# FFN first half by seven one-lane products in Strassen's way, with V fetched per step

## The chip, the cores and the metric

The kernel runs on one core of one Trainium2 chip. The time is the device time of one execution in microseconds (us); for the kernel before it is the median of three runs. TensorE (PE) multiplies, VectorE (DVE), ScalarE (ACT) and GpSimd (POOL) work on SBUF and PSUM, and SyncE (SP) issues nearly all DMAs.

## What is computed

```python
x = A_x                                   # 2048 x 512, fp32
g = sigmoid((x * gate_w).sum(-1))
qkv = x @ wqkv                            # 32 heads of 16
p = softmax(q @ k.T / 4); o = p @ v       # per head, no mask
a = o @ wo
h = silu(x @ w1) * (x @ w3)               # 2048 x 1792
b = h @ w2
out = g * a + (1 - g) * b
```

All is fp32. The projections and the FFN split each operand into a rounded part (hi) and the rest (lo), and sum three products: hi x hi, lo x hi and hi x lo.

## The kernel before

A first phase of 85 us loads and transposes x, projects the first q and k and all of V, and computes a bound for the softmax. V stays in SBUF for all heads. Then comes one long loop over 1024 score units. A unit is two heads, 128 keys and 512 queries: two matmuls into PSUM (L719), one exp on ACT (L723), and later four matmuls of P times V into four column groups of one bank (L706). A step is the 32 units of one head pair and one half of the queries; after it `evac` copies the bank (L687) and SP stores eight pieces (L693, L700). There are 64 steps.

The order of PE's work is a string written out by hand. Q is a score; F is a slot for two filler matmuls, one on rows 0 to 63 of the array (the upper lane) and one on rows 64 to 127 (the lower lane); P is one unit's PV part, 4 matmuls of 2 heads each taking the time of some slots. A long period is `"QFFF" * 7 + "QPPPP"` (8 scores, 21 slots), and there are 83 of them; a short one is `"QFFF" * 5 + "QPPQQPP"` (8 scores, 15 slots, PV in two pairs), and there are 44. Positions below are counted in such periods.

The fillers are the rest of the kernel, taken in order from `blocks`: the projections of the other q and k, gate and up of the FFN (`w_product`, L409), the second half of the FFN (`h_product`, L518), and part of the output projection (L597). A block has 12 lane matmuls on each lane for K = 512 (four K tiles, three terms), and both lanes sum into one bank: the upper lane takes the first 64 rows of every K tile, the lower lane the other 64. An FFN chunk is one group of 128 columns f of w1 and of w3; it makes eight blocks (gate and up for four blocks of 512 tokens).

When a gate block is done, DVE copies it (L432), ACT takes exp at the next P (L437), and DVE adds one (L438) and takes eight reciprocals (L440), a few per score. The up block is multiplied by the gate (L454), and by the reciprocals (L458), and SP stores that to `h_d` (L459). Weights are loaded by SP (L314) and split by POOL with a cast (L321) and a subtraction (L322). `load_w2` and `load_piece` bring w2 and h back (L487), and POOL splits these too (L488, L489). SP runs its DMAs in program order, so a store that waits for its data holds up every load behind it.

## Time and profile before

| | |
|---|---|
| median of three runs | 1419.17 us (1418.86 to 1424.47) |
| the profiled execution | 1419.55 us |
| its span | 1417.6 us |
| mean granted clock of PE | 1.0 |
| PE, ACT, DVE, POOL busy | 1408.8, 1033.2, 449.4, 321.1 us |
| bytes moved | 141.42 MB in 112668 packets |

A page of the profile gives the busy time of each engine over the span, the chain of work that ended last, and groups of instructions by line with their mean duration, the idle time before them and what ended it. A timeline row gives start and duration in us, the engine, the line, the operation with its tiles, and in brackets the idle time before it. A row of windows gives the stretch, its length, the busy time of PE, PEld, DVE, ACT and POOL, then the granted clock, the DMA share and GB/s. A row of the chain gives start, length, engine and line. A row of waits gives who waited for whom: the total in us, how often, and the longest.

### The profile page before, as it was taken

The page shows a single profiled execution, that of the slowest core. Times are in us where ns is not written, and L with a number is a line of the kernel's source. Part 1 is how long each engine was busy: PE and PEld are TensorE (multiplying, and loading weights), DVE is VectorE, ACT ScalarE, POOL GpSimd, SP SyncE. Part 2 cuts the span into 40 slices and gives each one's busy share as a digit, 9 for nine tenths or more (in the row PEclk, how much of TensorE's full clock was granted, in tenths as well). Part 3 has the DMA queues.
Part 4 walks back from the last instruction along what each step waited for, and adds up shares of the span by engine and source line. Part 5 has one row for each costly group of instructions (what it writes and reads, how often), then busy time and mean ns, then how long its engine had stood idle before and what let it go on. Part 6 is the DMA issues. An engine that isn't in the chain of part 4 may idle for free.

```text
span 1417.6 us, 28518 instructions
## 1 busy us (share of the span) xinstructions
PE 1408.8 (99%) x11399; PEld 833.7 (59%) x11399; DVE 449.4 (32%) x845; ACT 1033.2 (73%) x1153; POOL 321.1 (23%) x356
## 2 busy tenths in 40 slices
PE   9999999999999999999999999999999999999998
PEld 7865656656556566565565665655555555554556
DVE  4421102464555545455464545400000000000013
ACT  4556767777777777777777777777788778877870
POOL 5014443011011100110110015441332332233230
PEclk9999999999999999999999999999999999999999
DMA  7554455342124432223233234543534443345445
GB/s 197 141 121 114 126 140 128 73 110 69 46 61 85 113 69 61 70 72 87 68 76 79 76 81 122 136 101 74 126 81 102 104 105 70 66 112 106 106 133 182
DMA packets 112668, 141.42 MB, mean 100 GB/s; under 512 B 16400, under 2 KB 70672, under 8 KB 109456
## 3 DMA queue, kind: packets, MB, share of 16 engines
q1 hardware_dynamic: 110384, 135.72, 39.6%
q10 hardware_dynamic: 2144, 3.80, 0.8%
q8 instruction: 92, 1.51, 0.5%
q14 instruction: 48, 0.39, 0.1%
HBM read 90.70 MB, written 48.76 MB: 98 GB/s over the span
## 4 chain that ended last, share of the span: by engine, by line
PE 93%; POOL 0%; DMA 0%; DVE 0%; ACT 0%; issue 0%; SPq 0%; ACTq 0%; POOLq 0%
PE acc L706 32%; PE f L409 27%; PE S L719 19%; PE f L518 11%; PE f L597 1%; PE f L95 0%; PE f L97 0%; PE f L96 0%; DMA fr<-in_B_w_dram 0%; PE S L97 0%; PE S L96 0%; PE S L95 0%; POOL xL L489 0%; POOL fl L489 0%; DVE sg L458 0%; POOL xH L488 0%
## 5 line engine op out<-in xcount | busy, mean ns | idle before, releaser
L723 ACT ACTIVATE p<-S 128x1024 f32<-128x1024 f32 x1024 | 967.5, 1026 | 308.4 <-PE S L719 307.1
L706 PE MATMUL acc<-p,V 128*17 128x512 f32 x4096 | 473.5, 594 | 0.0
L719 PE MATMUL S<-Qt,Kt 50*128 50x512 f32 x2048 | 427.9, 413 | 1.1 <-POOLq L278 0.6
L719 PEld LDWEIGHTS S<-Qt,Kt 50*128 50x128 f32 x2048 | 193.8, 184 | 187.4 <-ACT p L723 80.4
L706 PEld LDWEIGHTS acc<-p,V 128*17 128x17 f32 x4096 | 102.8, 97 | 274.1 <-issue 273.9
L409 PE MATMUL f<-xL,fh 64*128 64x512 f32 x1024 | 205.1, 391 | 0.0
L409 PE MATMUL f<-xH,fl 64*128 64x512 f32 x1024 | 204.9, 390 | 0.0
L409 PE MATMUL f<-xH,fh 64*128 64x512 f32 x1024 | 204.7, 390 | 0.0
L440 DVE RECIPROCAL sg<-sg 128x64 f32<-128x64 f32 x448 | 201.2, 509 | 1.9
L409 PEld LDWEIGHTS f<-xL,fh 64*128 64x128 f32 x1024 | 99.4, 187 | 21.2
L409 PEld LDWEIGHTS f<-xH,fl 64*128 64x128 f32 x1024 | 98.5, 185 | 20.1
L409 PEld LDWEIGHTS f<-xH,fh 64*128 64x128 f32 x1024 | 99.4, 187 | 17.7
L321 POOL CAST fh<-fr 128x512 fp32r<-128x512 f32 x32 | 21.6, 674 | 371.1 <-DMA fr<-in_B_w_dram 246.5
L687 DVE COPY u<-acc 128x512 f32<-128x512 f32 x32 | 22.1, 692 | 257.0 <-PE acc L706 257.0
L518 PE MATMUL f<-xH,fl 64*128 64x512 f32 x224 | 82.2, 391 | 0.5 <-POOL fl L489 0.5
L518 PE MATMUL f<-xL,fh 64*128 64x512 f32 x224 | 82.2, 391 | 0.3 <-POOL xL L489 0.3
L518 PE MATMUL f<-xH,fh 64*128 64x512 f32 x224 | 82.1, 391 | 0.0
L518 PE MATMUL f<-xH,raw 64*128 64x512 f32 x192 | 74.9, 390 | 0.0
L532 DVE TENSOR_SCALAR gs<-f,omg 128x512 f32<-128x512 f32 x16 | 12.0, 751 | 176.4 <-PE f L518 176.4
L432 DVE COPY gs<-f 128x512 f32<-128x512 f32 x56 | 38.7, 691 | 78.1 <-PE f L409 78.1
L518 PE MATMUL f<-xH,fr 64*128 64x512 f32 x160 | 62.4, 390 | 0.0
L454 DVE TENSOR_TENSOR raw<-f,gs 128x512 f32<-128x512 f32 x50 | 34.1, 682 | 82.7 <-PE f L409 82.7
(216 smaller groups left out, 1309.6 us busy)
## 6 DMA issues: line engine op xcount, KB each, us to landing
Kt<-kH_d SPq DMA_DIRECT2D x128, 128.0 KB
h_d<-sg SPq DMA_DIRECT2D x56, 256.0 KB
sg<-h_d SPq DMA_DIRECT2D x43, 256.0 KB
fr<-in_B_w_dram SPq DMA_DIRECT2D x42, 256.0 KB
Qt<-qH_d SPq DMA_DIRECT2D x128, 64.0 KB
Kt<-kL_d SPq DMA_DIRECT2D x64, 128.0 KB
fr<-in_A_wqkv_dram SPq DMA_DIRECT2D x18, 256.0 KB
Qt<-qL_d SPq DMA_DIRECT2D x64, 64.0 KB
```

The source lines that it names most:

```text
L321: nc.gpsimd.tensor_copy(wh, r)
L409: nc.tensor.matmul(ps, w[i == 2][r, k, :], (xL if i == 1 else xH)[b][r, k, :], start=n == 0 and r.start == 0, stop=n == 3 * ND - 1 and r.s ...
L432: nc.vector.tensor_copy(gs, ps)
L440: small.append(lambda q=q: nc.vector.reciprocal(sg[:, q:q + 64], sg[:, q:q + 64]))
L454: nc.vector.tensor_mul(gu, ps, st["gs"])
L518: nc.tensor.matmul(ps, hs[t][q][i == 2][r, P * o:P * o + P], (w2L if i == 1 else w2H)[q][r, o, :], start=n == 0 and r.start == 0, stop=n = ...
L532: nc.vector.tensor_scalar(y, ps, omg[:, t:t + 1], None, op0=OP.mult)
L597: nc.tensor.matmul(ps, ot[t][i == 2][r, P * k:P * k + P], wo_[k][i == 1][r, :], start=n == 0 and r.start == 0, stop=n == 3 * ND - 1 and r. ...
L687: nc.vector.tensor_copy(u, acc)
L706: nc.tensor.matmul(acc[r:r + DH + 1, :], V[:, k, 2 * j + h, :], p[:, h, :], start=k == 0, stop=k == NT - 1)
L719: nc.tensor.matmul(ps[:, h, :], Kt[i][r:r + 50, P * k:P * k + P], Qt[i][r:r + 50, t:t + 512], start=True, stop=True)
L723: nc.scalar.activation(p, ps, AF.Exp, scale=SCALE)
```

## The change

The eight one-lane products of a chunk and a pair of token blocks (two token blocks, gate and up, two halves of each K tile) become seven products of sums, 12 lane matmuls each. Every product stands on one lane alone: `f_job` (L631 in the changed kernel) gives four products of a chunk to one lane and three to the other, in turn. There are 28 chunks now: 14 groups of columns for tokens 0 to 1023, then the same for tokens 1024 to 2047. Lane matmuls of the first half go from 2688 to 2352. `chunk_load` issues six loads for a chunk (L593 to L595), a half of them into the other partitions; `chunk_sums` makes four sums on POOL (L602) and `chunk_split` four casts (L617) and four subtractions (L619). Sums of x are made once per half by `x_sums` on DVE and split on POOL (L497, L498); those of the later half wait in DRAM (`X_d`). The outputs are put together on DVE from PSUM (`p1_done` to `p4_done`); the two products of the activation (L673, L687) are on POOL, and the store of h (L688) is on SP.

V goes to DRAM in the first phase (`keep_v`); `load_v_step` (L246) fetches a head pair for each step, 14 scores ahead of it. Pools of tiles are laid out anew. The projections come in another order, w2 is loaded when the last chunk's products end (`f_job`), into the tiles that x leaves, and `h_product` (L765) is emitted when the load of its row of w2 has been emitted. The first half's divisions come later. Of the 127 periods 71 are long; the other 56 have 13 or 14 slots.

```diff
-    V = vp.tile([P, NT, H, DH + 1], F32, name="V")
+    Vt = [vp.tile([P, NT, 2, DH + 1], F32, name=f"Vt{i}") for i in range(2)]
+    ones = const.tile([P, H], F32, name="ones")
     Qt = [qkp.tile([P, S // 2], F32R, name=f"Qt{i}") for i in range(2)]
...
+    def keep_v(t, e):
+        nc.gpsimd.tensor_copy(Vt[0][:, t, :, :], Vs[t][:, 0:2, :])
+        e.dma_start(V_d[t], Vs[t])
...
+    def load_v_step(s):
+        j = s % NPAIR
+        nc.sync.dma_start(Vt[s % 2], V_d[:, :, 2 * j:2 * j + 2, :].rearrange("t p h d -> p t (h d)"))
...
+    def x_sums(half, k):
+        b = 2 * half
+        m, ms = raw(), raw()
+        for i in range(2):
+            nc.vector.tensor_add(m[:, i, :], xH[b + i][:, k, :], xL[b + i][:, k, :])
+        yield
+        nc.sync.dma_start(ms[LO], m[UP])
+        nc.sync.dma_start(ms[UP, 1, :], m[LO, 1, :])
+        for _ in range(3):
+            yield
+        s1, s3 = slot("sg"), slot("sg")
+        nc.vector.tensor_add(s1, m[:, 1, :], ms[:, 1, :])
+        nc.vector.tensor_sub(s3[UP], m[UP, 0, :], m[UP, 1, :])
+        yield
+        nc.vector.tensor_sub(s3[LO], ms[LO, 1, :], ms[LO, 0, :])
+        nc.vector.tensor_add(m[LO, 0, :], m[LO, 0, :], ms[LO, 0, :])
+        yield
+        nc.vector.tensor_sub(m[:, 0, :], s1, m[:, 0, :])
+        yield
+        return s1, m[:, 0, :], s3
...
+    def first_half():
+        assert "saved" in free_x
+        for k in range(ND):
+            s1, s2, s3 = yield from x_sums(0, k)
+            if k == ND - 1:
+                prepare(0)
+            x_split(s1[UP], xH[2][UP, k, :], xL[2][UP, k, :])
+            yield
+            x_split(s3, xH[3][:, k, :], xL[3][:, k, :])
+            yield
+            t = slot("AC"[k % 2], F32R), slot("BD"[k % 2], F32R)
+            x_split(s2, *t)
+            yield
+            for i, xs in enumerate((xH, xL)):
+                nc.sync.dma_start(xs[2][LO, k, :].bitcast(F32), t[i][LO].bitcast(F32))
+            upper_s2.append(t)
+            if 1 in free_x:
+                put_s2()
+        x_there.update((1, 3))
+        for n in (0, 1, 3, 2):
+            chunk_split(chunks[0], n)
+        second_chunk()
...
+    def second_chunk():
+        if 0 in free_x and "a" in chunks[0]:
+            prepare(1)
+            for n in (0, 1, 3, 2):
+                chunk_split(chunks[1], n)
...
+    def chunk_load(c):
+        a, b = raw(), raw()
+        c["a"], c["b"] = a, b
+        for i, w in enumerate((w1, w3)):
+            w = w[:, P * c["f"]:P * c["f"] + P].rearrange("(k p) n -> p k n", p=P)
+            to = lambda t: t[:, i, :].rearrange("p (k n) -> p k n", n=P)
+            nc.sync.dma_start(to(a), w)
+            nc.sync.dma_start(to(b)[UP], w[LO] if i else w[UP])
+            nc.sync.dma_start(to(b)[LO], w[UP])
+    def chunk_sums(c):
+        a, b = c["a"], c["b"]
+        def step(op, to, x, y):
+            def go():
+                op(to, x, y)
+                c["t"] += 1
+            return go
+        sub, add = nc.gpsimd.tensor_sub, nc.gpsimd.tensor_add
+        poolq.extend([step(sub, b[LO, 0, :], a[LO, 0, :], b[LO, 0, :]),
+                      step(sub, b[:, 1, :], b[:, 1, :], a[:, 1, :]),
+                      step(sub, a[UP, 1, :], a[UP, 1, :], a[UP, 0, :]),
+                      step(add, b[:, 0, :], b[:, 1, :], b[:, 0, :])])
+    def chunk_split(c, n):
+        def hi():
+            assert c["t"] == 4
+            c[n] = halves()
+            nc.gpsimd.tensor_copy(c[n][0], src)
+        def lo():
+            nc.gpsimd.tensor_sub(c[n][1], src, c[n][0])
+            c["is", n] = True
+        src = (c["a"], c["a"], c["b"], c["b"])[n][:, (0, 1, 0, 1)[n], :]
+        poolq.extend([hi, lo])
...
+    def f_job(i, n, lane, done, when=None):
+        c = chunks[i]
+        def product(ps, r, m):
+            k, j = divmod(m, 3)
+            nc.tensor.matmul(ps, c[n][j == 2][r, P * k:P * k + P], (xL if j == 1 else xH)[XT[n]][r, k, :],
+                             start=m == 0, stop=m == 3 * ND - 1)
+        def end(ps):
+            done(c, ps)
+            if lane is LO or n == 3:
+                if i + 2 < len(chunks):
+                    chunk_split(chunks[i + 2], n)
+                else:
+                    t = i + 2 - len(chunks)
+                    loads.append(lambda q=len(asked[t]): load_piece(t, q))
+                    asked[t].append(n)
+            if c["half"] == 0 and c["f"] >= NF - (2 if n == 3 else 1):
+                x_from(n, lane)
+            if (c["half"], c["f"], lane) == (1, NF - 1, LO):
+                w = (0, 1, 3, 2)[n]
+                loads.extend([lambda f=f: load_w2(f) for f in range(4 * w, min(4 * w + 4, NF))])
+        def begin():
...
-                nc.vector.tensor_mul(sg, gu, sg)
-                nc.sync.dma_start(h_d[P * f:P * f + P, 512 * b:512 * b + 512], sg)
...
-            if f == NF - 1:
-                loads.extend([lambda c=c: load_w2(c) for c in range(4 * b, min(4 * b + 4, NF))])
-                if b == NB - 1:
-                    loads.extend([lambda q=q: load_piece(1, q) for q in range(2)])
-                    hurry = True
...
+            hurry = hurry or i == len(chunks) - 1
+            if n == 0 and lane is UP and i + 2 < len(chunks):
+                chunk_load(chunks[i + 2])
+            c[n, lane is LO] = True
+            if n == 2 and lane is UP and i + 2 < len(chunks):
+                chunk_sums(chunks[i + 2])
...
+        def silu():
+            nc.gpsimd.tensor_mul(c["sg", b], c["sg", b], gs)
+            ready_h(c, b)
+        soon.append(exp)
+    def ready_h(c, b):
+        c["n", b] = c.get(("n", b), 0) + 1
+        if c["n", b] == 2:
+            poolq.append(lambda: h_out(c, b))
+    def h_out(c, b):
+        sg, f, t = c["sg", b], c["f"], 2 * c["half"] + b
+        h = sg if b else c["up", b]
+        nc.gpsimd.tensor_mul(h, c["up", b], sg)
+        nc.sync.dma_start(h_d[P * f:P * f + P, 512 * t:512 * t + 512], h)
...
+    def p1_done(c, ps):
+        c["A"] = slot("A")
+        nc.vector.tensor_copy(c["A"], ps)
+    def p2_done(c, ps):
+        nc.vector.tensor_add(c["A"], ps, c["A"])
+        assert "B" in c
+        gate(c, 0, c["A"])
+    def p6_done(c, ps):
+        c["B"] = slot("B")
+        nc.vector.tensor_add(c["B"], ps, c["A"])
...
     def load_w2(f):
         if f % 4 == 0:
-            w2H.append(xp.tile([P, 4, 512], F32R, name=f"xH{f // 4}"))
-            w2L.append(xp.tile([P, 4, 512], F32R, name=f"xL{f // 4}"))
-        halves_of(w2[P * f:P * f + P, :], w2H[-1][:, f % 4, :], w2L[-1][:, f % 4, :], "fr")
+            w2H.append(xp.tile([P, 4, 512], F32R, name=f"xH{(0, 2, 3, 1)[f // 4]}"))
+            w2L.append(xp.tile([P, 4, 512], F32R, name=f"xL{(0, 2, 3, 1)[f // 4]}"))
+        halves_of(w2[P * f:P * f + P, :], w2H[-1][:, f % 4, :], w2L[-1][:, f % 4, :], "ww")
+        w2_there.append(f)
...
-    LONG, MID = 83, 0
+    LONG, MID = 71, 28
...
-    two = ["QFFF" * 5 + "QPPQQPP", "QFFF" * 6 + "PPQQPP"]
+    two = ["QQFFFFFQFFFQFFFFFQQPPQQPP", "QFFQFFFFQFFFQFFFFQFQPPQQPP"]
...
+            if issued % 32 == 18 and step < 2 * NPAIR:
+                load_v_step(step)
```

Two places of the new order, the first on SP and POOL. On SP where the FFN begins: `ww` tiles with 64- or 128-row sources from w1 and w3 are the first chunk's operands (`ww_7548`, `ww_7549`), `ww_7531` a block of k, `u` the evacuation of a step.

```order
480 L956 DMA d_d_89<-u_7509 1x512 x4
481 L963 DMA o_d_87<-u_7509 16x512 x4
482 L199 DMA kH_d_83<-ww_7531 128x512
483 L199 DMA kL_d_84<-ww_7531 128x512
484 L565 DMA xH1_236<-A_7076 64x512
...
489 L565 DMA xL1_237<-B_7402 64x512
490 L593 DMA ww_7548<-in_B_w1_dram 128x4x128
491 L594 DMA ww_7549<-in_B_w1_dram 64x4x128
492 L595 DMA ww_7549<-in_B_w1_dram 64x4x128
493 L593 DMA ww_7548<-in_B_w3_dram 128x4x128
494 L594 DMA ww_7549<-in_B_w3_dram 64x4x128
495 L595 DMA ww_7549<-in_B_w3_dram 64x4x128
```

The same weights were two loads per chunk before; here the six loads stand behind two stores of k, eight stores of the evacuation and six moves of sums of x (L565).

On POOL, what stands ahead of the first chunk's first operand, `wt_7637`, of which PE takes the rounded part first (the first product, `f0_7743<-xH0_154,wt_7637`, stands six scores into period 13):

```order
161 L602 TENSOR_TENSOR ww_7549<-ww_7548,ww_7549 64x512
162 L497 CAST xH3_611<-sg_7476 128x512
163 L498 TENSOR_TENSOR xL3_612<-sg_7476,xH3_611 128x512
164 L602 TENSOR_TENSOR ww_7549<-ww_7549,ww_7548 128x512
165 L497 CAST C_7584<-ww_7418 128x512
166 L498 TENSOR_TENSOR D_7585<-ww_7418,C_7584 128x512
167 L602 TENSOR_TENSOR ww_7548<-ww_7548 64x512
168 L461 CAST ww_7625<-ww_7625 128x512
169 L462 TENSOR_TENSOR ww_7625<-ww_7625 128x512
170 L602 TENSOR_TENSOR ww_7549<-ww_7549 128x512
171 L617 CAST wt_7637<-ww_7548 128x512
172 L619 TENSOR_TENSOR wt_7637<-ww_7548,wt_7637 128x512
```

Before, POOL had a cast and a subtraction for each of two tiles at this place (L321, L322); now four sums (L602), the sums of x (L497, L498), a block of k (L461, L462) and the split stand in one row.

On SP where the second half begins, before (`fr` tiles hold rows of w2 or pieces of h):

```order
728 L487 DMA fr_14809<-in_B_w2_dram 128x512
729 L487 DMA fr_14850<-in_B_w2_dram 128x512
730 L487 DMA fr_14884<-in_B_w2_dram 128x512
731 L459 DMA h_d_86<-sg_14729 128x512
732 L487 DMA fr_14913<-in_B_w2_dram 128x512
733 L487 DMA fr_14944<-h_d_86 128x4x128
734 L487 DMA fr_14987<-h_d_86 128x4x128
735 L487 DMA fr_15020<-in_B_w2_dram 128x512
736 L459 DMA h_d_86<-sg_14876 128x512
737 L487 DMA fr_15052<-in_B_w2_dram 128x512
738 L487 DMA fr_15079<-in_B_w2_dram 128x512
739 L487 DMA fr_15122<-in_B_w2_dram 128x512
```

and now, where `ww` tiles hold them and `sg_15491`, `D_15579` and `sg_15789` are products of h of the last two chunks:

```order
936 L688 DMA h_d_86<-sg_15491 128x512
937 L734 DMA ww_15569<-in_B_w2_dram 128x512
938 L734 DMA ww_15588<-in_B_w2_dram 128x512
939 L734 DMA ww_15604<-in_B_w2_dram 128x512
940 L734 DMA ww_15621<-in_B_w2_dram 128x512
...
945 L734 DMA ww_15707<-in_B_w2_dram 128x512
946 L688 DMA h_d_86<-D_15579 128x512
947 L734 DMA ww_15727<-in_B_w2_dram 128x512
...
955 L734 DMA ww_15853<-in_B_w2_dram 128x512
956 L688 DMA h_d_86<-sg_15789 128x512
957 L734 DMA ww_15867<-in_B_w2_dram 128x512
```

The loads of w2 and the stores of h stood mixed over several periods before; now the first load of w2 (row 0) stands behind the store of `sg_15491`, that of row 7 behind the store of `D_15579`, and that of row 13 behind the last store.

On PE the first product that needs row 0 of w2 (`f1_15592<-xH0_15567`, L765) stands one score behind that load in the order of the program; products of the last chunk (L631) run beside it on the other lane, as L409 ran beside L518 before.

More of the change, by code (lines that the diff above doesn't have):

```diff
@@ new lines, in both, with prepare @@
+    def both(*a):
+        upper.append(block(*a))
+        lower.append(upper[-1])
+    def prepare(i):
+        chunk_load(chunks[i])
+        chunk_sums(chunks[i])
+    for c, b in [(c, b) for b in (2, 3) for c in (1, 2, 3)] + [(1, 1), (1, 0), (2, 1), (3, 1), (2, 0), (3, 0)]:
+        for i in range(2):
+            begin = None
+            if (b, i) == (2, 0) and c < ND - 1:
+                begin = lambda c=c: load_weights(c + 1)
+            both(w_product(c, i, b), qk_done(c, i, b), 3 * ND, begin)
@@ L683, in feed @@
+            t["n"] += 1
+            if t["n"] == t["length"]:
+                now[name] = None
+                if t["two"] and name == "upper":
+                    t["up"] = issued
+                else:
+                    t["done"](t["ps"])
+                    ended += 1
+                    left_at[t["bank"]] = clock
         return did
@@ L770, in gated_mix_kernel @@
     assert not pend and issued == 64 * NPAIR
-    assert state_f["upper"] is None and all(b[0] < issued for b in ready)
+    assert not upper and now["upper"] is None and all(t["up"] < issued for t in lower)
     for _ in reciprocals(ND - 1, 1):
```

400 lines of the change are left out of this document (227 added, 173 removed).

## The prediction

> **What bounds the kernel now.** I read the page first, then the chain of waits, then timelines of a long period, a short period and the stretch where the first half of the FFN ends, and last the waits of SP.
>
> ```profile
> span 1417.6 us, 28518 instructions
> PE 1408.8 (99%) x11399; PEld 833.7 (59%) x11399; DVE 449.4 (32%) x845; ACT 1033.2 (73%) x1153; POOL 321.1 (23%) x356
> PE 93%; POOL 0%; DMA 0%; DVE 0%; ACT 0%; issue 0%; SPq 0%; ACTq 0%; POOLq 0%
> L723 ACT ACTIVATE p<-S 128x1024 f32<-128x1024 f32 x1024 | 967.5, 1026 | 308.4 <-PE S L719 307.1
> ```
>
> PE is the bound: busy 99% of the span, 93% of the chain, and ACT idles 308 us waiting for it. So the time is a count of matmul slots times their length, plus whatever makes PE wait. The run that was profiled took 1419.55 us around its span of 1417.6; the median of the three runs is 1419.17, 0.4 below.
>
> A period is 8 scores with the fillers between them. The chain shows the PV blocks, one to a long period:
>
> ```profile
> 104.75 3.56 PE acc L706 x32
> ...
> 241.07 3.56 PE acc L706 x32
> ```
>
> Between them lie 13 periods in 136.32 us: 10.49 each. The slot is read from a timeline of PE:
>
> ```profile
> 602.14 0.40 PE L409 MATMUL f<-xH,fh 64*128 64x512 f32 x2
> 602.38 0.40 PE L409 MATMUL f<-xL,fh 64*128 64x512 f32 x2
> 602.61 0.40 PE L409 MATMUL f<-xH,fl 64*128 64x512 f32 x2
> 602.85 0.40 PE L719 MATMUL S<-Qt,Kt 50*128 50x512 f32 x2
> ...
> 603.78 0.40 PE L719 MATMUL S<-Qt,Kt 50*128 50x512 f32 x2
> ```
>
> Four slots take 0.93 us, so a slot (a pair of fillers, or a score) takes 0.2325. A long period has 8 scores and 21 fillers: 29 x 0.2325 = 6.74, and the rest, 3.75, is the PV block. The exps beside two PV pairs give a short period:
>
> ```profile
> 1099.93 1.94 ACT L723 ACTIVATE p<-S 128x1024 f32<-128x1024 f32 x2 [1.25 <-PE S L719]
> 1109.35 1.94 ACT L723 ACTIVATE p<-S 128x1024 f32<-128x1024 f32 x2 [1.25 <-PE S L719]
> ```
>
> The start of the second row is 9.42 us after the first: 23 slots are 5.35, the PV part 4.08.
>
> **The change part by part.** *PE work.* 83 long and 44 short periods become 71 long, 28 of 21 slots and 28 of 22. Removed: 12 x 10.49 + 44 x 9.43 = 540.8. Added: 28 x (21 x 0.2325 + 4.08) + 28 x (22 x 0.2325 + 4.08) = 28 x 8.96 + 28 x 9.20 = 508.5. The gain is 32.3 us (29 to 34: some of the new periods start with two scores in a row). ACT needs 8 x 1.026 = 8.2 us of 8.96, so it does not become the bound there. Seven products for eight alone would be an eighth of the first half; the fillers that remain set the rest.
>
> The old kernel loses some time itself where the second half starts:
>
> ```profile
> 911.60:934.10 22.50, 21.73 (x160) 12.61 (x161) 1.06 (x2) 15.47 (x18) 10.31 (x12) 1.00 0.31 87
> ```
>
> Two periods and a bit take 1.5 us more than 2 x 10.49. This place is rebuilt, so these 1.5 us go and new waits come.
>
> *Durations off PE.* The new sums, splits and products run on GpSimd (POOL) and stand behind DMAs of SP:
>
> ```profile
> L422 POOL TENSOR_TENSOR gs<-gs,sg 128x512 f32<-128x512 f32 x24 | 30.9, 1289 | 1.9
> L421 POOL CAST sg<-gs 128x512 fp32r<-128x512 f32 x24 | 14.7, 612 | 82.5 <-DVE gs L420 82.5
> L440 DVE RECIPROCAL sg<-sg 128x64 f32<-128x64 f32 x448 | 201.2, 509 | 1.9
> L432 DVE COPY gs<-f 128x512 f32<-128x512 f32 x56 | 38.7, 691 | 78.1 <-PE f L409 78.1
> L438 DVE TENSOR_SCALAR sg<-sg 128x512 f32<-128x512 f32 x56 | 27.1, 484 | 103.0 <-ACT sg L437 103.0
> L437 ACT ACTIVATE sg<-gs 128x512 f32<-128x512 f32 x56 | 35.0, 625 | 0.0
> ```
>
> Between two POOL instructions lie 0.07 us, as the chain shows where two follow each other:
>
> ```profile
> 916.79 0.62 POOL xH L488
> 917.41 0.07 issue
> 917.48 1.28 POOL xL L489
> ```
>
> Two loads show what a load costs from its issue on SP to the cast on POOL:
>
> ```profile
> 198.47 1.03 SPq L314 DMA_DIRECT2D fr<-in_B_w_dram  x2
> ...
> 202.48 0.61 POOL L321 CAST fh<-fr 128x512 fp32r<-128x512 f32 x1 [4.41 <-DMA fr<-in_B_w_dram]
> ```
>
> ```profile
> 889.12 0.37 SPq L487 DMA_DIRECT2D fr<-in_B_w_dram  x1
> 891.79 0.61 POOL L488 CAST xH<-fr 128x512 fp32r<-128x512 f32 x1 [11.98 <-DMA fr<-in_B_w_dram]
> ```
>
> So 4.0 us for the weight columns (x2 issues in 1.03) and 2.7 for a row block of w2; one issue takes about 0.4.
>
> *Start of the FFN.* The six loads of the first chunk (after's L593 to L595) are behind two stores of k, eight evacuations and six moves of x sums. From the first score of that period: 3.75 (PV) + 0.9 + 0.7 (copy) + 16 issues x 0.4 + three of the chunk's own (1.2) + 4.0 = 17 us until the first sum can run; then POOL does eight tensor-tensors and four casts up to the first low part: 8 x 1.29 + 4 x 0.61 + 12 x 0.07 = 13.6. The high part is there after 17 + 12.2 = 29.2. PE meets its first product (L631) one period and 6 scores later: 10.49 + 3.75 + 5 x 0.93 + 2 x 0.23 = 19.4. It waits 29.2 - 19.4, about 9.5 us, and 0.5 at a later operand: 10 (6, if the evacuations are issued while SP would otherwise wait, to 12).
>
> *Second chunk.* Its loads follow the last k store out of the same buffer: copy 0.7, three POOL instructions 3.3, two issues 0.8, the store 2.7 (as the w2 row), six issues 2.4, landing 4.0, three sums 4.1, cast 0.7: 18.7 us after the last projection product. PE wants it 13.5 us after (one period and 13 slots): a wait of 5 (2 to 8).
>
> *End of the FFN's first half.* Before, most loads of w2 are issued periods ahead, and yet one of them already ended in the chain, behind a store of h:
>
> ```profile
> 909.52 0.69 DVE hx L454
> 910.21 0.47 DVE sg L440
> ...
> 910.70 1.28 DVE sg L458
> ...
> 912.00 0.32 SPq L459
> ...
> 912.42 4.25 DMA fr<-in_B_w_dram
> ```
>
> ```profile
> SPq L459 <- DVE sg L458: 336.9, 49, 10.6
> ```
>
> SP stood up to 10.6 us at such a store. In the changed kernel all fourteen loads of w2 come after the last jobs of the lower lane, and the loads of rows 0, 7 and 13 each stand directly behind an h store (L688). A store waits for: exp of the score 1.3 and of the gate 0.6, tensor_scalar 0.5, eight reciprocals 4.1 with three or four subtractions of w2 or h (0.7 each) between them, two POOL products and a cast with their gaps 3.4: 12 us after the score that the gate's exp follows. Then 0.4 issue, 2.7 to 4.25 landing, 0.6 cast: 16 to 17.3. The first product of h (L765) that needs the row stands 3.75 + 4 x 0.93 + 2 x 0.23 = 7.9 us behind that score, the third one group less, 7.0. Waits: 6.5 for row 0 (5.7 to 7.3: no subtraction stands between its reciprocals), 8.5, 8.5. They add up, as each gate's exp is behind a score that PE issues only after the wait before. Sum 23.5 (12 if the loads land at once and the reciprocals run without a subtraction between; 30 with 4.25 each).
>
> *Clock.* The waits are long enough for the clock gate to matter. After the last matmul:
>
> ```profile
> 1412.00:1414.00 2.00, 1.45 (x7) 0.87 (x5) 2.00 (x4) 0.00 (x0) 0.00 (x0) 1.00 0.99 384
> 1414.00:1416.00 2.00, 0.00 (x0) 0.00 (x0) 0.24 (x1) 0.00 (x0) 0.00 (x0) 1.00 0.92 354
> 1416.00:1417.60 1.60, 0.00 (x0) 0.00 (x0) 0.00 (x0) 0.00 (x0) 0.00 (x0) 0.75 0.00 0
> ```
>
> With PE idle the granted clock goes from 1.00 to 0.75 over the last 1.6 us: to half, some 3 us after the last matmul. All five waits are longer. How long the clock stays low afterwards no row shows; I take the same 3 us at half rate, 1.5 us each, 7.5 in all (0 to 10). The Trainium skill, "TensorE: Matmul & The Clock Gate", section "Why this matters for your kernels", warns of gaps of PE over about 3 us between bursts, which the last row agrees with; by the 3.4 us of its table in Part 1 I would estimate 1.7 each, 8.5.
>
> *Steady state of the first half.* A chunk is 84 lane products, 42 slots of fillers, two long periods: 20.98 us. POOL does 12 tensor-tensors and 4 casts per chunk: 12 x 1.289 + 4 x 0.612 + 16 x 0.07 = 19.0. Beside a DVE operation on two SBUF tiles a cast of 0.61 took 1.07:
>
> ```profile
> 877.15 0.82 DVE L458 TENSOR_TENSOR sg<-hx,sg 128x512 f32<-128x512 f32 x1
> 877.37 1.07 POOL L488 CAST xH<-fr 128x512 fp32r<-128x512 f32 x1
> ```
>
> Two such DVE operations are left per chunk, and two tensor_scalars: 2 x 0.46 and at most as much again. POOL is then at 20 to 20.8 of 20.98: full, but it just keeps up. Term 0, with up to +15 as a rival. DVE has 16 reciprocals (8.1) and some 12 others (8.5): 16.7, no bound.
>
> *V per step.* 64 loads of 2048 pieces of 136 B.
>
> ```profile
> q1 hardware_dynamic: 110384, 135.72, 39.6%
> ```
>
> A packet there takes 0.396 x 1417.6 x 16 / 110384 = 81 ns on average; by that a load of V takes 128 x 81 ns = 10.4 us on each engine, by bytes a ninth of it. It is issued 14 scores before its step, 15 us or more, so it is hidden; 0, or some us at single chunk loads behind it. The chunk loads (28 MB instead of 7) add 21 MB to 141, hidden too. The moved division and the staged V before the loop: 0 (-2 to +3).
>
> Sum: 1419.55 - 32.3 - 1.5 + 10 + 5 + 23.5 + 7.5 = 1431.75; less the 0.4 to the median, 1431.
>
> **The rivals.** *The queues don't bind* (faster). If the loads at the three places arrive before PE asks, only the first term is left: 1419.2 - 33.8 = 1385; with half of the waits 1405. For it speaks that before has only 1.5 us lost at a place built alike, though SP waits there for 336.9 us in all; against it, that before's loads of w2 were spread over three periods and only the last ones stood behind a store, while now row 0 is issued one score ahead of its product. The point from which it decides: the store must be ready 5 us earlier. Chance 0.22 for under 1410, and 0.17 for 1410 to 1420.
>
> *GpSimd becomes the bound.* If a chunk takes POOL 21.5 instead of 20.98, 26 chunks lose 13 us beyond a slack of some 10 us: 1431 + 3 to 1431 + 20. The threshold is 0.98 us of added contention per chunk. The Trainium skill, "SBUF — State Buffer", section "SBUF: two separate sides", calls the port that the two engines share an exclusive lock held for the whole instruction. The pair of rows agrees in part, as the cast lost 0.46 of the 0.60 that both ran; by the lock each meeting would cost a full DVE operation of 0.69. Chance 0.14.
>
> *The change's slots are not saved* (the new periods run into ACT or PE stays at the old length): 8.2 of 8.96 us leaves 0.7 per period, so I give it 0.03, at 1445 to 1460.
>
> **How the numbers follow.** The forecast, 1420 to 1446, has 0.44; the three rivals 0.22 + 0.17, 0.14 and 0.03. From 1402 to 1452 lie 8 in 10: below it is the rival in which nearly all waits vanish, above it most of a GpSimd that falls behind. A measurement of this kernel tells 0.5% apart, 7 us: faster is under 1412, slower over 1426. Of the forecast's 0.44 some 0.06 lies under 1426; with 0.22 and a sliver of the 0.17 faster gets 0.25, same 0.20, slower 0.55.
>
> **What would show it.** PE's waits at L631, twice near the fourteenth to sixteenth period, and three at L765 near the seventieth, with SP standing at L688 before w2; a granted clock under 1.00 in those stretches; PE's busy time down to 1375 or so with idle time up to 40; long periods between them still 10.49. It is wrong if those five waits sum to less than 20 us, or if periods in the middle of the first half are longer than 10.6, POOL being late.

## The result, and the profile after

The changed kernel takes 1557.19 us, the median of four runs (1553.96 to 1560.13); the kernel before took 1421.36 beside it (1418.86 to 1424.47). The ratio is 1.0954, with a 95% interval from 1.0919 to 1.0989: 136 us slower. The forecast was slower, at 1431, with eight chances in ten from 1402 to 1452; the direction held, and the size is out by 126 us.

The top of the page after, with busy time, share and count of each engine, and two rows of its 40 slices:

```profile
span 1558.3 us, 28947 instructions
PE 1444.2 (93%) x11063; PEld 822.3 (53%) x11063; DVE 578.4 (37%) x1009; ACT 1046.0 (67%) x1153; POOL 804.6 (52%) x805
PE   9976897689999999699999985899999999999999
PEclk9978999889999999899999997799999999999999
```

Two things are to be seen. PE issues 336 matmuls fewer than before and is yet busy 35 us longer. And its clock, 9 in every slice before, dips only in slices where PE has gaps: the mean granted clock is 0.955, so 0.045 x 1558 = 70 us of full speed are missing. PE idles 114 us instead of 9.

The same stages of both kernels, each from one first exp of a period to another: up to period 0, then to periods 13, 20, 40, 46, 67, 73 and 127, and the tail. The columns are the stretch, its length, the busy time of PE, PEld, DVE, ACT and POOL with the number of instructions, the granted clock, the DMA share and GB/s. Before:

```profile
0.00:86.20 86.20, 82.80 (x389) 66.96 (x390) 38.22 (x73) 35.48 (x72) 25.25 (x38) 1.00 0.65 165
86.20:219.30 133.10, 132.59 (x1123) 80.59 (x1122) 16.59 (x24) 97.62 (x104) 49.38 (x53) 1.00 0.48 122
219.30:293.00 73.70, 73.70 (x634) 44.08 (x632) 28.29 (x54) 54.85 (x62) 12.24 (x13) 1.00 0.41 90
...
502.80:565.80 63.00, 63.00 (x542) 37.40 (x540) 30.94 (x63) 47.69 (x54) 3.75 (x4) 1.00 0.33 73
...
786.60:849.60 63.00, 63.00 (x544) 37.72 (x542) 32.38 (x63) 47.82 (x55) 5.04 (x5) 1.00 0.32 78
849.60:1373.70 524.10, 523.33 (x4296) 280.74 (x4292) 61.68 (x106) 413.20 (x439) 176.79 (x198) 1.00 0.44 104
```

And after:

```profile
0.00:97.60 97.60, 83.64 (x388) 67.33 (x389) 36.81 (x73) 35.25 (x72) 28.97 (x69) 0.96 0.67 183
97.60:280.40 182.80, 150.53 (x1121) 88.96 (x1122) 60.62 (x80) 100.71 (x105) 93.72 (x95) 0.90 0.64 163
280.40:381.60 101.20, 81.96 (x622) 46.71 (x618) 38.53 (x64) 55.62 (x61) 75.98 (x72) 0.88 0.59 128
381.60:594.00 212.40, 212.40 (x1804) 126.35 (x1806) 149.26 (x277) 161.90 (x182) 185.00 (x162) 1.00 0.53 112
594.00:680.00 86.00, 71.74 (x543) 42.61 (x541) 45.04 (x84) 49.29 (x56) 53.84 (x49) 0.88 0.95 185
680.00:902.80 222.80, 222.73 (x1893) 132.69 (x1889) 155.05 (x289) 170.10 (x191) 190.10 (x167) 1.00 0.54 112
902.80:1013.30 110.50, 82.78 (x520) 42.21 (x517) 50.16 (x86) 49.69 (x54) 35.61 (x39) 0.78 0.34 86
1013.30:1516.50 503.20, 500.45 (x4000) 248.57 (x3998) 31.48 (x44) 414.52 (x433) 141.33 (x158) 1.00 0.53 114
```

The stages differ, after less before, by +11.4 (up to the loop), +49.7 (periods 0 to 13: k and q projections), +27.5 (13 to 20: the FFN begins), +2.6 (20 to 40), +23.0 (40 to 46: the change of halves), +2.0 (46 to 67), +47.5 (67 to 73: the second half of the FFN begins; 63.0 before, and 60.1 if the two short periods among them had the forecast length), -20.9 (73 to 127) and -2.1 in the tail: 140.7 in all. In the middle of each half of the tokens PE is busy all the time at a clock of 1.00, with POOL at 185 of 212 us: GpSimd keeps up. Nearly all the loss is at five changes of stage, and in each of them the clock is below 1.

### The profile page after: what moved, and what is told of

Its sections match the earlier page's. It is cut to its first block, busy times and chain, and to the rows that moved or that the text cites. A ratio compares the mean times of both kernels' runs of the same rounds, so it can differ in the third digit from the quotient of the medians.

```text
span 1558.3 us, 28947 instructions
## 1 busy us (share of the span) xinstructions
PE 1444.2 (93%) x11063; PEld 822.3 (53%) x11063; DVE 578.4 (37%) x1009; ACT 1046.0 (67%) x1153; POOL 804.6 (52%) x805
## 4 chain that ended last, share of the span: by engine, by line
PE 68%; DMA 10%; POOL 6%; SPq 4%; DVE 4%; issue 2%; ACT 0%; DVEq 0%; POOLq 0%; ACTq 0%
PE acc L969 24%; PE f L631 15%; PE S L982 15%; PE f L765 9%; DMA ww<-in_B_w_dram 2%; DMA xL<-x_d 2%; DMA Kt<-kL_d 1%; PE f L840 1%; PE f L450 1%; DMA ww<-ww 1%; SPq L297 1%; POOL ww L462 1%; DMA Qt<-qH_d 1%; DMA ww<-h_d 1%; SPq L290 1%
## 5 line engine op out<-in xcount | busy, mean ns | idle before, releaser
L969 PE MATMUL acc<-p,Vt 128*17 128x512 f32 x4096 | 485.8, 605 | 0.0
L631 PE MATMUL f<-xH,wt 64*128 64x512 f32 x1568 | 357.6, 407 | 36.6 <-POOL wt L617 17.2
L631 PEld LDWEIGHTS f<-xH,wt 64*128 64x128 f32 x1568 | 224.8, 192 | 72.9 <-POOL wt L617 18.1
L631 PE MATMUL f<-xL,wt 64*128 64x512 f32 x784 | 256.1, 402 | 6.6 <-DMA xL<-x_d 6.6
L969 PEld LDWEIGHTS acc<-p,Vt 128*17 128x17 f32 x4096 | 102.1, 98 | 275.8 <-issue 272.1
L765 PE MATMUL f<-xH,wt 64*128 64x512 f32 x896 | 205.3, 398 | 17.2 <-POOL xH L735 14.6
L735 POOL CAST wt<-sg 128x512 fp32r<-128x512 f32 (+1 forms) x60 | 33.7, 561 | 310.0 <-DMA sg<-h_d 220.6
L602 POOL TENSOR_TENSOR ww<-ww 64x512 f32<-64x512 f32 x112 | 148.1, 1330 | 58.8 <-DMA ww<-in_B_w_dram 53.6
L765 PE MATMUL f<-xL,wt 64*128 64x512 f32 x448 | 158.1, 401 | 3.5 <-DVE xL L736 3.5
L631 PEld LDWEIGHTS f<-xL,wt 64*128 64x128 f32 x784 | 147.6, 193 | 24.4 <-DMA xL<-x_d 8.4
L765 PEld LDWEIGHTS f<-xH,wt 64*128 64x128 f32 x896 | 131.4, 189 | 38.7 <-POOL xH L735 17.1
L619 POOL TENSOR_TENSOR wt<-ww,wt 128x512 fp32r<-128x512 f32 x112 | 147.0, 1313 | 8.9
L450 PE MATMUL f<-xH,wt 64*128 64x512 f32 x384 | 92.1, 434 | 32.3 <-DVE ww L460 32.2
L765 PEld LDWEIGHTS f<-xL,wt 64*128 64x128 f32 x448 | 84.3, 188 | 15.9 <-DVE xL L736 7.5
L617 POOL CAST wt<-ww 128x512 fp32r<-128x512 f32 x112 | 75.8, 677 | 26.5 <-PE f L631 26.5
L667 DVE TENSOR_SCALAR sg<-sg 128x512 f32<-128x512 f32 x56 | 39.5, 705 | 92.4 <-ACT sg L666 87.3
```

The lines of the kernel that those rows point to most:

```text
L450: nc.tensor.matmul(ps, w[i == 2][r, P * k:P * k + P], (xL if i == 1 else xH)[b][r, k, :], start=n == 0 and r.start == 0, stop=n == 3 * ND ...
L602: op(to, x, y)
L617: nc.gpsimd.tensor_copy(c[n][0], src)
L619: nc.gpsimd.tensor_sub(c[n][1], src, c[n][0])
L631: nc.tensor.matmul(ps, c[n][j == 2][r, P * k:P * k + P], (xL if j == 1 else xH)[XT[n]][r, k, :], start=m == 0, stop=m == 3 * ND - 1)
L667: small.append(lambda: nc.vector.tensor_scalar(sg, sg, 1.0, None, op0=OP.add))
```

## The experiments

Each kernel below ran once, with a profile. The changed kernel's own runs lie 6 us apart, so differences below that aren't read from whole times, and stages are compared instead. A single stage varies too: four kernels with the same code up to period 13 (the changed kernel and the three with late stores of h) took 182.8, 184.5, 186.8 and 186.2 us there. Spans: 1558.3 in the changed kernel, 1417.6 before.

**Without the later half's sums** (span 1505.4). `later_half` and the reload `x_from` are left out, so the second half of the FFN multiplies the first half's sums.

```diff
     def later_half():
-        for i, xs in enumerate((xH, xL)):
-            nc.sync.dma_start(X_d[0, 0, i], xs[2][:].bitcast(F32))
...
+        yield
         free_x["saved"] = True
...
-            if c["half"] == 0 and c["f"] >= NF - (2 if n == 3 else 1):
-                x_from(n, lane)
```

> The changed kernel without the sums of x of the later half of the tokens, and without their reload: the second half of the FFN multiplies the first half's sums. Theory A (the sums of x in the early loop block DVE and SP, and their reload fills the DMA engines at the half): the first 13 periods, 182.8 us in the changed kernel, fall to 140 or less, and the six periods from the 40th, 86.0, to 65 or less; about 65 us in all. Rival B (the loss there comes from V per step and from the other order of the projections): less than 15 us in all, the first 13 periods stay above 170.

Periods 0 to 13, and 40 to 46:

```profile
96.90:251.70 154.80, 144.22 (x1123) 86.10 (x1124) 38.88 (x52) 99.74 (x105) 68.52 (x71) 0.93 0.51 126
562.90:627.00 64.10, 63.54 (x544) 37.84 (x542) 44.62 (x84) 48.48 (x56) 54.59 (x49) 1.00 0.56 116
```

The change of halves goes from 86.0 to 64.1, at full clock: its 22 us are the reload, some 8 MB by the code, while the DMA engines were busy for 0.95 of the stage. The early loop gives back 28 us, less than the 42 expected: the earlier half's sums, from period 9 on, still cost their own.

**Without any sums of x** (span 1473.2). `later_half` and `x_from` are left out as in the run before, and `first_half` only prepares the chunks; the seven products run on plain x.

```diff
-        for k in range(ND):
-            s1, s2, s3 = yield from x_sums(0, k)
-            if k == ND - 1:
-                prepare(0)
...
+        yield
+        prepare(0)
```

> The changed kernel without any sums of x: nothing is summed, split, moved or reloaded, and all seven products of a chunk run on plain x (the FFN's first half is then another computation with as many matmuls). Theory A (the sums of x make the projections late): the first 13 periods, 154.7 us without the later half's sums alone, come down to 134 to 142, against 133.1 in the kernel before; and the first chunk is ready sooner, so that the next 7 periods fall from 99 to 90 or less. Rival B (V per step, SP's many DMAs and the order of the projections hold them up): the first 13 periods stay above 148.

Periods 0 to 13, and 13 to 20:

```profile
96.40:235.00 138.60, 138.28 (x1121) 83.97 (x1122) 16.92 (x25) 98.63 (x104) 58.35 (x64) 0.96 0.56 133
235.00:319.30 84.30, 77.08 (x624) 45.32 (x622) 37.22 (x64) 55.20 (x62) 57.29 (x54) 0.96 0.58 119
```

Theory A holds: 138.6 and 84.3 instead of 182.8 and 101.2. Making, storing and reloading the sums costs 85 us of span. V per step, the new order of the projections and the many loads are all still in this run, and cost at most 5.5 us in the first 13 periods. Even these 5.5 are accounted for: the clock is 0.50 in the first 11.0 us of the loop, behind PE's wait at the loop's start.

**More scores between move and use** (span 1545.3).

```diff
-        for _ in range(3):
+        for _ in range(7 if half else 3):
             yield
```

> The changed kernel with 7 instead of 3 scores between the move of a sum's half inside SBUF and the DVE operation that needs it, for the later half's sums alone. Theory A1 (DVE stands in order at that operation until the move has landed, and the evacuations of PE's banks stand behind it): the first 13 periods lose 20 to 45 us less than in the changed kernel. Rival A2 (SP, the DMA engines and the buffers are too loaded there in any order): less than 10 us less.

The first 13 periods take 175.6, so 7 less (7 to 11, by the four kernels above), where theory A1 has 20 to 45. DVE's waits at the operation that needs a moved half did fall, from 49.8 us between 98 and 240 us to 20.3, and PE got only a quarter of that back: theory A1 falls as the main cause. Another wait came in their place: DVE now stood 23.8 us at one copy behind POOL's split of weights (L349).

**Moves issued by ACT** (span 1561.7).

```diff
-        nc.sync.dma_start(ms[LO], m[UP])
-        nc.sync.dma_start(ms[UP, 1, :], m[LO, 1, :])
+        e = nc.scalar if half else nc.sync
+        e.dma_start(ms[LO], m[UP])
+        e.dma_start(ms[UP, 1, :], m[LO, 1, :])
...
-            nc.sync.dma_start(X_d[half - 1, n, i, lane, k, :], t[i][lane].bitcast(F32))
+            nc.scalar.dma_start(X_d[half - 1, n, i, lane, k, :], t[i][lane].bitcast(F32))
```

> The changed kernel with the moves inside SBUF and the stores of the later half's sums issued by ACT instead of SP. Theory S (SP's one queue makes the projections late: stores of k and q, loads of weights and of the next step stand behind the sums' moves): the first 13 periods, 182.8 us, fall by 15 to 35. Rival (the sums' operations on DVE and POOL stand in the way, whoever issues the moves, or ACT's exps get late for them): by less than 6, or they grow.

187.4 in the first 13 periods, against 182.8 to 186.8: SP's issue of these moves is not the narrow part.

**A fifth large buffer** (span 1559.1).

```diff
-        return fk.tile(list(shape), dtype, name=tag, bufs=3 if tag == "sg" else 2)
+        return fk.tile(list(shape), dtype, name=tag, bufs=2)
...
-        return fw.tile([P, 2, 512], F32, name="ww", bufs=4)
+        return fw.tile([P, 2, 512], F32, name="ww", bufs=5)
```

> The changed kernel with five instead of four of the large buffers that loads, sums of x and stores of k and q share, paid for with two instead of three small ones for gates. Theory A3 (the shared buffers set the early loss: a copy out of PE's bank waits until a store or a sum has left its buffer): the first 13 periods, 182.8 us, fall by 15 or more. Rival A2 (SP's queue sets it): by less than 6. The chunks in the middle can become slower for want of the small buffer.

185.6, and the change of halves grows from 86.0 to 93.8: theory A3 falls in this form. The sums take two of the small buffers as well, which are one fewer here, so it is not a clean test.

**The split of the weights later on POOL** (span 1544.9). What led to it is a timeline of the changed kernel, POOL and DVE in the third period of the loop, 27.0 us long:

```profile
122.70 0.61 POOL L348 CAST wt<-ww 128x512 fp32r<-128x512 f32 x1 [12.26 <-DMA ww<-in_A_wqkv_dram]
```

```profile
141.23 0.69 DVE L486 TENSOR_TENSOR sg<-ww 128x512 f32<-128x512 f32 x1 [11.26 <-DMA ww<-ww]
...
144.46 0.68 DVE L460 COPY ww<-f 128x512 f32<-128x512 f32 x1
```

SP sends the loads of the next step first (L297, from 108.4 us), then the weights (L139, at 117.3); POOL stands 12.3 us at their cast, and the splits of the sums and of k and q stand behind it; DVE then stands 11.3 us at a moved half, and the copy (L460) that would free PE's bank of PSUM stands behind that.

```diff
-                begin = lambda c=c: load_weights(c + 1)
+                begin = lambda c=c: weights_later(c + 1)
...
+    def weights_later(c):
+        w = [load_w(D * i + P * c).rearrange("p k n -> p (k n)") for i in range(2)]
+        wqk[c] = []
+        for i in range(2):
+            due.append((issued + 5 + i, lambda i=i: wqk[c].append(split(w[i]))))
```

> The changed kernel with the split of the second and third k and q weights five scores later on POOL than their loads on SP, instead of right behind them. Theory P (in the early loop POOL stands in order at that split until the weights land, up to 12 us, and the splits of the sums and of k and q behind it keep the shared buffers and PE's banks taken): the period of 27 us, the third, falls below 18, and the first 13, 182.8 us, by 8 to 20. Rival (each of the three queues holds the others up, and taking one wait out moves it elsewhere, as with the other three edits): the first 13 periods stay within 6 us.

The third period takes 18.2 and the first 13 take 174.3, 8.5 less (8.5 to 12.5, by the four kernels above). So this wait is one cause, with some 10 us; others take its place in part. Of the four edits that keep the sums, none gives back a quarter of the 50 us.

**Stores of h behind the loads of w2** (span 1545.3).

```diff
-        nc.sync.dma_start(h_d[P * f:P * f + P, 512 * t:512 * t + 512], h)
+        store = lambda: nc.sync.dma_start(h_d[P * f:P * f + P, 512 * t:512 * t + 512], h)
+        if hurry:
+            loads.append(store)
+        else:
+            store()
```

> The changed kernel with the stores of h of the last chunk put behind the loads of w2 that are pending, so that no load of w2 waits for the gate. Theory C (the three stores hold the loads up, as the prediction says): the waits of PE at the second half's first products fall from 25 us to 8 or less, and with the clock's share the six periods from the 67th, 110.5 us, fall by 30 to 45. Rival D (landing, buffers or POOL set these waits, the stores only coincide): by less than 12.

The six periods from the 67th take 97.0, 13.5 less than 110.5, between the two theories. Some of this is work put off: 20 matmuls of `h_product` that the changed kernel does in these periods come later here, and the tail is 3 us longer. The span as a whole is 13.0 us shorter. The timeline of POOL in this run shows why the rest stays (from L688 on, its line numbers, and those of the next two runs, are higher by four):

```profile
949.49 1.27 POOL L673 TENSOR_TENSOR sg<-sg,B 128x512 f32<-128x512 f32 x1 [4.94 <-DVE sg L669]
950.70 0.62 POOL L739 CAST wt<-ww 128x512 fp32r<-128x512 f32 x1
951.27 1.27 POOL L687 TENSOR_TENSOR sg<-C,sg 128x512 f32<-128x512 f32 x1
952.47 2.65 POOL L739 CAST xH<-ww 128x512 fp32r<-128x512 f32 x3
```

The casts of w2 come without a gap right behind the activation's products, which wait for the reciprocals. The rows of w2 had landed: the gate holds them up in POOL's queue as it did in SP's.

**Besides, the activation's products on DVE** (span 1536.8).

```diff
-            small.append(lambda: poolq.append(silu))
+            small.append(silu if hurry else lambda: poolq.append(silu))
...
-            nc.gpsimd.tensor_mul(c["sg", b], c["sg", b], gs)
+            (nc.vector if hurry else nc.gpsimd).tensor_mul(c["sg", b], c["sg", b], gs)
...
-            poolq.append(lambda: h_out(c, b))
+            (small if hurry else poolq).append(lambda: h_out(c, b))
```

(The product in `h_out` goes to DVE in the same way.)

> The run with late stores, and besides the two products of the activation of the last chunks on DVE, so that no cast of w2 stands behind them on POOL. Theory C2 (the gate holds w2 up twice, by the store on SP and by its product in POOL's queue, and either alone is enough): the six periods from the 67th, 97.0 us with late stores alone and 110.5 in the changed kernel, fall to 76 to 86. Rival D (DVE is the one that is late there, with eight reciprocals and the subtractions of w2 in one queue): they stay above 92.

91.6: another 5 us, and no more; theory C2 fails, and the time lies just under rival D's bound. Its waits name the third queue, with total, number and longest:

```profile
DVE wt L740 <- POOL wt L739: 35.5, 3, 19.1
...
PE f L631 <- DVE B L705: 4.6, 1, 4.6
```

DVE stands at a subtraction of h (L740) that waits for POOL's cast and so for a load, and the sum that takes a product out of PE's bank (L705) stands behind it.

**Besides, the subtractions back on POOL** (span 1529.3).

```diff
-        (nc.vector if hurry else nc.gpsimd).tensor_sub(lo, r[:, 0:n], hi)
+        nc.gpsimd.tensor_sub(lo, r[:, 0:n], hi)
```

> The run with late stores and the activation's products on DVE, and besides the subtractions of w2 and h back on POOL, as they are in the kernel before. Theory C3 (DVE's queue is the third that the loads hold up: a subtraction waits there for a load, and the copies out of PE's banks stand behind it): the six periods from the 67th, 91.6 us there and 110.5 in the changed kernel, fall to 72 to 82. Rival (a load is issued one score ahead of its product, and landing alone makes PE wait): they stay above 88.

84.8, between the two bounds. The three steps together, from 110.5 in the changed kernel:

```profile
905.00:1002.00 97.00, 76.75 (x499) 40.15 (x496) 50.15 (x86) 49.70 (x54) 36.27 (x38) 0.84 0.38 97
```

```profile
901.90:993.40 91.50, 75.61 (x499) 39.31 (x496) 50.49 (x94) 49.67 (x54) 24.37 (x30) 0.85 0.40 102
```

```profile
900.70:985.50 84.80, 72.91 (x499) 36.25 (x496) 41.41 (x74) 48.94 (x54) 49.04 (x50) 0.88 0.44 111
```

Half of the 50 us is order in three queues: on SP the stores of h ahead of the loads of w2, on POOL the gate's products ahead of the casts of w2, and on DVE the subtractions of h and w2 ahead of what takes products out of PE's banks. PE's idle time falls from 27.7 to 11.9, and the clock rises with it. The longest wait that is left is again for row 0 of w2:

```profile
PE f L769 <- POOL xH L739: 7.1, 2, 6.5
```

Its cast stands on POOL behind casts of h, and POOL waits 10.0 us for a load of h that SP sends behind the loads of the next step. No run takes this away.

**Even slots, and the first split back** (span 1556.5).

```diff
-    two = ["QQFFFFFQFFFQFFFFFQQPPQQPP", "QFFQFFFFQFFFQFFFFQFQPPQQPP"]
+    two = ["QFFFQFFFQFFFQFFQFFQPPQQPP", "QFFQFFFFQFFFQFFFFQFQPPQQPP"]
...
-    load_weights(1)
...
     load_guard(0, 0, 0)
+    load_weights(1)
```

> The changed kernel with the 13 slots of the shorter period spread evenly, no two scores in a row except at PV, and with the first split of k and q weights back behind the rows of the guard. Theory G (two scores in a row wait for the exp of the one before the last): the 54 periods after the 73rd, 503.2 us, fall by 5 to 8. Rival: 13 slots cost as much in any order, less than 2. Theory W (the early split on POOL delays V and the guard's rows): the loop's first exp, 97.6 us after the start, comes 5 to 10 us earlier. Rival (SP's loads of k and q set it): less than 3.

The 54 periods take 501.2 instead of 503.2, and the loop starts at 99.1: both rivals hold. The 2.0 us are no gain of the new order: the changed kernel has one wait of PE of 2.0 us there that this run lacks. Periods of 13 and of 14 slots both take 9.2 us, in either order of the 13. The timeline of ACT in the changed kernel shows what seems to set them:

```profile
1123.92 1.94 ACT L986 ACTIVATE p<-S 128x1024 f32<-128x1024 f32 x2 [0.83 <-PE S L982]
1126.43 3.78 ACT L986 ACTIVATE p<-S 128x1024 f32<-128x1024 f32 x4 [0.57 <-PE S L982]
1130.42 1.02 ACT L986 ACTIVATE p<-S 128x1024 f32<-128x1024 f32 x1 [0.22 <-PE S L982]
```

Around the PV pairs ACT runs out of scores, 0.83 + 0.57 + 0.22 = 1.6 us per period, and between them it works without a gap, 0.92 us an exp. 8 x 0.92 + 1.6 is 9.0: by this a period can't be much shorter, however few slots it has. This is a reading of the trace, and no run tests it.

**One wait by itself, four times** (span 1473.5) **and shorter** (1439.8). The kernel before, with POOL kept busy ahead of one weight tile of four chunks.

```diff
+    MORE = {5: 44, 7: 50, 9: 56, 11: 64}
...
-            nc.gpsimd.tensor_copy(wh, r)
+            for _ in range(1 + (MORE.get(chunks.index(chunk), 0) if n == "1" else 0)):
+                nc.gpsimd.tensor_copy(wh, r)
```

(The second run has 37, 33, 47 and 53.)

> The kernel before, with one of two weight tiles of four chunks cast 44, 50, 56 and 64 times more on POOL, so that PE waits once at each of four places, for some 1 to 20 us, and nothing else is changed. Theory E (each wait costs its own length and 1.5 us of low clock, as the prediction took): the period with the wait is longer by the wait and at most 2 us, and so are the two after it together. Rival F (after a wait the clock stays low for one or several fixed windows of 3.4 us, also after waits of 2 us): the sum of lost time is the wait and 1.7 to 7 us more, and a wait of 2 us can cost as much again.

> The kernel before with fewer additional casts at the four places, 37, 33, 47 and 53, for waits of some 1, 2, 3 and 4 us. If only a wait over 3 us lowers the clock, the first three periods are longer by the wait alone (within 0.3 us) and the last by some 2 us more; if shorter waits can lower it too, one of the first three is longer by 1.5 us or more beyond its wait.

Two of the periods with a wait in the first run, and three in the second:

```profile
431.91:459.02 27.11, 13.14 (x94) 7.17 (x96) 2.53 (x4) 7.63 (x10) 15.68 (x23) 0.75 0.07 23
543.00:566.11 23.11, 13.52 (x94) 7.88 (x92) 4.89 (x11) 8.34 (x11) 16.06 (x24) 0.78 0.28 47
```

```profile
314.89:327.82 12.93, 11.04 (x94) 6.17 (x92) 6.55 (x13) 8.15 (x10) 11.88 (x18) 1.00 0.06 22
422.27:438.75 16.48, 14.03 (x94) 7.26 (x96) 2.52 (x4) 7.61 (x9) 5.24 (x6) 0.79 0.12 37
522.66:540.16 17.50, 13.31 (x94) 7.93 (x92) 4.89 (x11) 8.33 (x10) 11.15 (x16) 0.80 0.37 61
```

A period is 10.49. With 14.0 us of waiting it took 27.1, 2.6 beyond the wait; with 9.6 us, 23.1, 3.0 beyond; the other two waits of this run, 6.2 and 11.7 us, cost 2.0 and 2.6 beyond. In the second run 1.9 us of waiting, in two pieces, left the clock at 1.00 and cost 0.5 beyond; 2.45 us lowered it to 0.79 and cost 3.5 beyond, 6.0 in all, so it doesn't take a wait of over 3 us; two waits of 4.2 us cost 2.8 beyond each. So a single wait costs itself and 2.0 to 3.5 us, whether it is 2.45 or 14 us long: rival F.

No length of wait that is safe follows from this. At the loop's start of the first run, where nothing was added, two gaps of PE of 0.9 and 0.5 us were followed by a clock of 0.50 for some 10 us, and the first 13 periods took 137.8 instead of 133.1; the kernel before has gaps of 0.6 and 0.5 us there and stays at 1.00. In the changed kernel a gap of 2.0 us at 1174.8 us was followed by 0.79 (mean of 1174 to 1182), and one of 2.0 us at 262.4 by 1.00 (262 to 277).

## Why the prediction was wrong, step by step

PE's waits in the changed kernel, in total, number and longest:

```profile
PE f L450 <- DVE ww L460: 32.2, 12, 9.7
PE f L631 <- POOL wt L617: 17.2, 2, 10.4
PE f L765 <- POOL xH L735: 14.6, 5, 7.2
PE S L982 <- SPq L314: 9.0, 1, 9.0
PE f L631 <- DMA xL<-x_d: 6.6, 4, 2.1
PE f L631 <- DMA xH<-x_d: 5.2, 2, 4.9
PE f L631 <- DVE A L692: 5.0, 1, 5.0
PE f L631 <- DVE B L701: 4.5, 1, 4.5
PE f L765 <- DVE xL L736: 3.5, 5, 1.3
```

**The five waits were there, and others beside them.** It named PE's waits at the FFN's start and at the first products with w2. At the start, the row of POOL instructions that it counted ran as counted: from the first sum, at 288.1 us, to the end of the first cast (L617) is 11.3 us, where it had 12.2 by 7 tensor-tensors and 4 casts. PE's two waits for these operands are 10.4 and 6.8, where it had 10 and 5; the whole stage idles 19.2. At w2 the stage idles 27.7, but only 18 of it is at products with w2 (L765, for L735 and L736): 7.8 at rows 0 and 1, 5.4 at rows 6 to 8, 4.8 at rows 12 and 13, where it had 6.5, 8.5 and 8.5. The other 9.5 are products of the last chunks (L631) that wait for a copy and a sum on DVE (L692, L701), each right behind a subtraction of h; with the subtractions back on POOL (span 1529.3) these two waits fall to 0.6 in all. SP shows the store and the loads behind it:

```profile
949.66 0.34 SPq L688 DMA_DIRECT2D h_d<-sg  x1
950.04 1.87 SPq L734 DMA_DIRECT2D ww<-in_B_w_dram  x4
```

The mechanism was right but not whole: POOL's queue holds w2 up behind the same gate, and DVE's holds up the last chunks' products, which had no term.

**The clock, mis-sized.** It priced five waits at 1.5 us, 7.5 in all, taking the low clock to last 3 us. In the two stages it spoke of, a clock of 0.88 over 101 us and 0.78 over 110.5 miss 12 and 24 us; in the whole span 70. Two reasons: the price of a single wait is 2.0 to 3.5, and PE has 28 gaps of over 1 us, not five. The rule of the Trainium skill, "TensorE: Matmul & The Clock Gate", section "Why this matters for your kernels", to leave no gap over about 3 us, held as a warning; in this case 2.45 us was enough. By its 3.4 us the estimate was 1.7 for each; measured was 2.0 to 3.5.

**The early loop, not priced.** The step that failed is the list of terms. "The moved division and the staged V before the loop: 0 (-2 to +3)" was all it had for the time before period 13. That the sums of x run there, on DVE and POOL, over SP and beside the projections, has no term at all; they cost 44 us in periods 0 to 13 (182.8 with them, 138.6 without), and 17 of the 27.5 behind. Of the 49.7 us that periods 0 to 13 grew, 32 are PE's waits for one copy on DVE (L460), and the rest is the clock, 0.90 on average. The work of the sums was small (DVE 60.6 of 182.8 us), and so PE would not be thought to wait; but in the timelines each engine takes its instructions in order, and a copy that frees a bank of PE stood behind an operation that waits for a transfer. (GpSimd touches tiles in SBUF alone in these traces; what leaves PSUM goes through DVE or ACT.) Removal of the sums shows the cause; which of the waits carries what share stays open but for the weights' split (8.5 to 12.5 us) and the distance of the moves (7 to 11).

**The change of halves, not priced.** Its text spoke of 21 MB of chunk loads, "hidden too", and not of the 8 MB of sums that SP loads again between 593 and 652 us. PE waits 11.8 us for them (`xL<-x_d`, `xH<-x_d`), and the stage grows by 23 us; 22 of it go in the run without them.

**The gain, mis-sized.** 32.3 us, with 29 as its lower bound, counted on 9.08 us for a short period, the mean of 8.96 and 9.20; both kinds take 9.2: some 8 us less, 24 in all. "ACT needs 8 x 1.026 = 8.2 us of 8.96" is an average over the period; by the timeline ACT stands idle for 1.6 us around PV, and works without a gap in the rest.

**The start of the loop**, +11.4 us. PE waits 9.0 us for SP, which reaches the branch at the loop's start (L314) later, and the clock is then 0.50 for the loop's first 12.3 us. Moving the first split of weights did not help. With a fifth large buffer the loop started at 93.9 us, against 95.9 to 99.1 in the changed kernel and the nine others made from it, so the shared buffers seem to have a part in it; the rest stays open.

**What held.** POOL at 185 of 212 us keeps pace, as the term 0 said, and the rival in which it falls behind did not come. The periods in the middle take 10.62 us on average, just over the 10.6 that was named as a sign of late POOL, but PE idles 0.02 us in all twenty of them, so it isn't that: most take 10.5, and every fourth, one in each step, 10.8 or more. Whether V per step makes this 0.3 us no run shows. The rival on the other side, waits that don't bind, is out.

Sum of the misses: 11.4 + 49.7 + 23 that had no term, about 9.5 more at the FFN's start (27.5 against 15 and 3 of clock), about 22 more at its second half (50.4 against 23.5 and 4.5), 8 of gain and 4.6 in the middle: in all 128, where the median was 126 above the forecast (the profiled run lies 3 us above the median).

## What to carry to other kernels

When work is moved onto engines with much idle time, follow it queue by queue at every change of stage: an instruction that waits for a transfer or a chain blocks all that stands behind it, the copy that frees an accumulator above all, and so a total of 37% busy says nothing. Price each single wait of TensorE of over 2 us with 2 to 3.5 us on top, take none for free because it is short, and list everything that the change adds, also where it runs long before the part that it is for. A saving of one product in eight was 24 us here; the sums that it needs cost 85.

## What the runs showed of the hardware that was not expected

A single wait of 2.45 us of TensorE halved its clock for 6.8 us (0.51 over this stretch of the run with the shorter waits), and the price beyond the wait did not grow with it, 2.0 to 3.5 us for waits of 2.45 to 14 us:

```profile
424.00:430.80 6.80, 6.08 (x28) 1.84 (x32) 0.00 (x0) 1.02 (x1) 3.64 (x4) 0.51 0.05 16
```

PE works for 6.1 of these 6.8 us, so most of the low clock falls behind the wait. Where gaps follow one another a whole stage stays low: 0.78 over 110 us at the second half's start.
